# Feeding an attention stage up to eight units ahead, around the window in which expert weights arrive

## The chip, the cores and the metric

The kernel runs on one core of a Trainium2 chip. The metric is the device time of one execution in microseconds, the median over several executions of the same program.

## The reference

A linear attention with a decaying state (batch 4, 8 heads, 768 tokens, head size 48) is followed by a mixture of experts that sends every token to one of 8 experts (384 to 1024 to 384). Cut to what matters:

```python
for t in range(S):                                   # attention, state is (B, H, D, D)
    cur = einsum('bhd,bhe->bhde', u * k[t], v[t])
    y[t] = einsum('bhd,bhde->bhe', r[t], state + cur)
    state = w[:, :, None] * state + einsum('bhd,bhe->bhde', k[t], v[t])
x = y as (B*S, H*D)                                  # 3072 tokens of 384
e_idx = argmax(x @ w_gate + modality_bias[modality_id])
out[token] = gate[token] * (relu(x[token] @ w1[e]) @ w2[e])   # e = e_idx[token]
```

## The kernel before

**Units.** The attention works on 24 units of 128 tokens: unit i is batch `i % 4` of chunk `i // 4`. The main loop has one pass (step) for each unit, and several units are in flight in it. In step i TensorE forms the scores of unit i+1 (`scores`, `psc`, line 416), the outputs of unit i (`values`: `py` and the state's update `pst`, lines 446 to 464) and the bonus of unit i+1 (line 385). VectorE (DVE) prepares the keys of unit i+2 (`keys`, `kc`, line 376), masks the scores of unit i+1 (`causal`, line 422), and adds, scales and splits the output of unit i-1 (`token`, `low`, lines 472 and 521). ScalarE (ACT) and GpSimd (POOL) take other parts, and SyncE (SP) issues nearly all DMAs. All five engines run in program order, since the whole stage is written under a manual schedule.

**Feeds.** Each unit needs r and k with head dimensions on the partitions (`turned`, a DMA into one of four buffers `ud`, each with a half for r and a half for k, 192 KB a half) and k and v with tokens on the partitions (`lines`, a DMA of 384 KB into one of five buffers `kv`). For units in `TURNED`, 1 to 13, `turned` loads r alone; `keys_turned` gets the turned k by four TensorE transposes of the `kv` buffer into a PSUM tile `pkT` (line 339), which `keys` and nothing else then reads in the loop. In step i the kernel issues `turned(i + 5)` and `lines(i + 4)`, each behind a `pace`: SP reads a value that an engine has just made, so that the DMA is not issued before that time.

**Expert weights beside it.** From step 8 on the first expert's weights (3 MB) arrive in six pieces of 512 KB (`piece`, line 881, `raw`): three at the end of step 8, and one at the end of each of steps 9, 10 and 11. ACT sums their squares (`norm`), a small matmul adds these up (`scales`, `pww`, line 898; its result lies in the one-buffer PSUM pool that `pst` also uses), and the pieces are split into two half-precision parts, `whi` by ACT (line 914) and `wlo` by DVE (line 919): piece 0 at the end of step 11, pieces 1 and 2 at the end of step 12, pieces 3 to 5 at the end of step 13. From step 13 on every second step begins a tile of 128 tokens for that expert: `s_up` multiplies by `w1` (`phs`, line 973) in two halves, ACT and DVE turn each half into `hh` and `hl` (`s_high` line 977, `s_low` line 982), and in the next step `s_down` multiplies by `w2` (`pos`, lines 1047 and 1052), and ACT takes the result (line 933).

**PSUM.** The pool `ps_a` has four buffers of one bank. The transposed keys `pkT`, the two score tiles of a unit, both halves `phs` and `pos` all come from it in turn, each waiting until the tile that had its buffer four tiles ago has been read.

**After the loop** the remaining tiles go through the experts in a loop of jobs (from line 1397), which takes the span from about 200 us to its end.

In step i, the order of the calls that matter here is: feeds (step 0 only), `keys_turned(i+2)`, `scores(i+1)`, the first half of `s_up` or `s_high` and the first half of `s_down`, `token(i-1)`, `taken(i)`, `turned(i+5)`, state, `s_low` of the second half, `decay(i+3)`, `carry(i+2)`, `keys(i+2)`, `factor(i-1)`, `lines(i+4)`, `causal(i+1)`, `low(i-1)`, `values(i)`, the second half of `s_up` or `s_down`, logits and planned work (weight pieces, `norm`, splits).

Of the kernel before, what the change touches and what calls it, by code (L numbers as in the profile page):

```python
# [9 lines left out]
F32 = mybir.dt.float32  # L10
# [11 lines left out]
NPR = H // 2  # L22
NT = B * S
DM = H * D
# [6 lines left out]
WC = DC * F  # L31
# [11 lines left out]
DENSE = 6  # L43
FADED = range(4, 14)
SHARED = range(9, 14)
TURNED = range(1, 14)

NE = 9
EARLY = 3
# [8 lines left out]
LOW, TOP = 64 - D, 64 + D  # L58
# [3 lines left out]
class _Kernel:  # L62
# [251 lines left out]
    def turned(self, i):  # L314

        b, c = self.units[i]
        n = NPR * P
        ud = self.ud[i % len(self.ud)]
        m = n if i in TURNED else 2 * n
        self.nc.sync.dma_start(ud[LOW:TOP, :m], self.pd[b * NCH + c].rearrange("j d n -> (j d) n")[:, :m])  # L320
        self.ctx_.setdefault(i, {}).update( rT=ud[:, :n].rearrange("p (a t) -> p a t", a=NPR), kT=ud[:, n:].rearrange("p (a t) -> p a t", a=NPR))

    def lines(self, i, q=None):

        b, c = self.units[i]
        u = self.ctx_.setdefault(i, {})
        u["kz"] = self.kv[i % len(self.kv)]
        kv = u["kz"][:, LOW:]
        qs = slice(0, 2) if q is None else slice(q, q + 1)
        self.nc.sync.dma_start(kv.rearrange("p (q d) -> p q d", q=2)[:, qs], self.pt[b * NCH + c].rearrange("p (q d) -> p q d", q=3)[:, ::2][:, qs])  # L330
        u.update(k=kv[:, :DM], v=kv[:, DM:])

    def keys_turned(self, i):

        if i in TURNED:
            u = self.ctx_[i]
# [723 lines left out]
    def run(self):  # L1060
        nc, tc, m = self.nc, self.tc, self.m
        units = self.units = [(b, c) for c in range(NCH) for b in range(B)]
        NU = len(units)
# [14 lines left out]
        self.wf = m.tile([P, 1], F32, name="wf", bufs=1)  # L1078
        self.meta = m.tile([P, 2], F32, name="fac", bufs=1), m.tile([P, 2], I32, name="ids", bufs=1)
        self.mt, m2 = [m.tile([P, 2, 4], I16, name=f"mt{q}", bufs=1) for q in range(2)]  # L1080
        self.slot = {}
        junk = m.tile([P, WQ], F16, name="junk", bufs=1)
        groups = {}
# [15 lines left out]
        def chain(*gs):  # L1099
            for g in gs:  # L1100
                yield from g
# [37 lines left out]
        def route(i, d, f, *args):  # L1139
            for lo, hi in GROUPS:  # L1140
                if hi - 1 + d == i and lo in groups:
                    f(groups[lo], *args)

        def each(i, *fs):
            for f in fs:
                if live(i):
                    f(i)


        def fill(n=1):  # L1150
            while n and fills:
                g = fills.pop(0)
                if next(g, fills) is not fills:
                    fills.append(g)
                    n -= 1

        for i in range(NU - 1):
            if i == 0:
                each(i + 5, self.turned)
                each(i + 4, self.lines)  # L1160
            each(i + 2, self.keys_turned)
            each(i + 1, self.scores)
            if i + 1 > EARLY:
                each(i + 1, self.own_keys)
            route(i, 3, lambda u: fills.append(self.choose(u)))
            route(i, 5, lambda u: fills.append(chain(self.place(u), self.ahead(ahead[u["lo"]], u)) if u["lo"] in ahead else self.place(u)))
            up, down = ups.get(i), ups.get(i - 1)
            if up is not None:
                self.s_up(up, 0)
            if down is not None:  # L1170
                self.s_high(down, 1)
                self.s_down(down, 0)
            self.token(i - 1) if i else None
            if ups.get(i - 2) is not None:
                self.s_take(ups[i - 2])
            if i and i - 1 == self.grp["lo"]:
                groups[i - 1] = self.grp
            fill()
            each(i, self.taken) if i else None
            each(i - 1, self.settled_state)  # L1180
            if 0 < i < NU - 5:
                self.pace(self.ctx_[i]["d"])
                each(i + 5, self.turned)
            for j in range(2):
                each(i - 1, lambda i: self.state(i, j))
                fill()
            if down is not None:
                self.s_low(down, 1)
                self.s_due(down)
            begin.get(i, lambda: None)()  # L1190
            late = i >= NU - 3
            for k in range(1 if late else 2):
                for d in (6, 7):
                    route(i, d, self.send, 1)
                if k == 0:
                    each(i + 3, self.decay)
            if ups.get(i - 2) is not None:
                self.s_give(ups[i - 2])
            each(i + 2, self.carry)
            route(i, 4, self.sign)  # L1200
            each(i + 2, self.keys)
            if i + 2 <= EARLY:
                self.own_turned(i + 2)
            if i:
                fac = self.factor(i - 1)
                for _ in fac:
                    fill()
                if i < NU - 4:
                    self.pace(self.ctx_[i - 1]["g"]["sx"][:, self.ctx_[i - 1]["at_g"] :])
                    each(i + 4, self.lines)  # L1210
            self.own(i, 0)
            each(i - 1, self.high)
            mid.get(i, lambda: None)()
            for j in range(2):
                each(i + 1, lambda i: self.causal(i, j))
                fill()
            self.own(i, 1)
            if late:
                for d in (6, 7):
                    route(i, d, lambda u: (self.rest(self.ctx_[i]["dv"][:1, DM - 1 :]), self.send(u, 1)))  # L1220
            each(i - 1, self.low)
            if up is not None:
                self.s_high(up, 0)
                self.s_low(up, 0)
            fill()
            each(i - 1, self.flip)
            fill()
            self.values(i)
            if up is not None:
                self.s_up(up, 1)  # L1230
            if down is not None:
                self.s_down(down, 1)
            for p in range(2):
                for h in range(2):
                    c, r = divmod(i + 1 - 2 * p - h, B)
                    if r == 0 and 0 < c < NCH - 1:
                        self.fade(c, slice(2 * p, 2 * p + 2), range(2 * h, 2 * h + 2))
            if any(hi - 1 + d == i for lo, hi in GROUPS for d in (4, 5)):
                fill(99)
            route(i, 2, self.logits)  # L1240
            route(i, 4, self.count)
            for f in at.get(i, ()):
                f()
            for k in turns.get(i, ()):
                self.s_turn(k)
# [4 lines left out]
        i, j = NU - 2, NU - 1  # L1250
# [206 lines left out]
```

## Time and profile before

| | |
|---|---|
| median of 3 runs | 359.08 us (358.05 to 360.82) |
| the profiled execution | 358.22 us, its span 356.4 us |
| PE (matmul) busy | 337.7 us, 95% |
| PEld (weight load) busy | 273.0 us, 77% |
| DVE busy | 221.8 us, 62% |
| ACT busy | 173.4 us, 49% |
| POOL busy | 153.7 us, 43% |
| mean granted TensorE clock | 0.979 |

The span runs from the first to the last instruction. Rows of a timeline give the start in us from the span's start, the length in us, the engine, the line of the program, the operation, and what it writes and reads (buffer numbers left out); instructions of one kind that follow one another are merged, with their count behind an x. A bracket at the end gives the idle time ahead of it and what ended it. Rows of a list of waits give who waited, for whom, the total in us, how often, and the longest. Ends of matmuls are modelled. A share of busy time is a mean over stages with different limits.

### The profile page before, as it was taken

To read this page: it belongs to the slowest core of one execution; us is meant where nothing else is said; L and a number is where in the kernel's file an instruction comes from. 1 tells how busy PE (TensorE), PEld (TensorE's weight loads), DVE (VectorE), ACT (ScalarE), POOL (GpSimd) and SP (SyncE) were. 2 spreads that over 40 slices of the span, in tenths; PEclk is the share of its full clock that TensorE was granted. 3 is DMA by queue.
4 is the path that set the end of the run, shared out by engine and by line. 5 is a ranking of instruction groups with operands and counts; after the bars stand their busy time and mean duration, and the time that the engine had idled before them with its cause. 6 is when DMAs were issued, how large, how long until landed. Compare 5 with 4: busy or idle time off the path is not lost. (4 is left out here: it accounts for less than half of the span.)

```text
span 356.4 us, 15193 instructions
## 1 busy us (share of the span) xinstructions
PE 337.7 (95%) x5453; PEld 273.0 (77%) x5453; DVE 221.8 (62%) x745; ACT 173.4 (49%) x459; POOL 153.7 (43%) x231
## 2 busy tenths in 40 slices
PE   8999999799899999999998999998999999999893
PEld 3888998698769788887876777775788887777671
DVE  7978999489797978684658632258223232323850
ACT  8677675646847648465531122255222224552911
POOL 8986868646646765342267311112111210211121
PEclk9999999858999999999999999999999999999999
DMA  6875769999739998572335531126621121112110
GB/s 180 231 172 149 173 141 289 246 260 219 188 112 205 253 275 218 110 183 82 69 113 180 203 67 44 44 59 208 209 60 44 44 60 29 44 44 66 32 47 4
DMA packets 60796, 47.72 MB, mean 134 GB/s; under 512 B 46920, under 2 KB 54359, under 8 KB 60496
## 3 DMA queue, kind: packets, MB, share of 16 engines
q1 hardware_dynamic: 57552, 37.65, 45.0%
q0 software_dynamic: 3200, 9.47, 7.6%
q8 instruction: 30, 0.49, 0.6%
q14 instruction: 14, 0.11, 0.1%
HBM read 25.83 MB, written 11.83 MB: 106 GB/s over the span
## 5 line engine op out<-in xcount | busy, mean ns | idle before, releaser
L973 PEld LDWEIGHTS <-whi 128*128 128x128 f16 x1248 | 72.4, 98 | 4.0 <-issue 1.0
L1047 PEld LDWEIGHTS <-hh 128*128 128x128 f16 x416 | 37.4, 98 | 36.0 <-ACT hh L977 9.9
L973 PE MATMUL phb<-mxT,whi 128*128 128x128 f16 x768 | 50.8, 219 | 0.0
L402 ACT ACTIVATE dv<-kv,d 128x48 f32<-128x48 f32 x172 | 43.1, 325 | 3.9 <-issue 2.2
L977 ACT ACTIVATE hh<-phb 128x256 f16<-128x256 f32 (+1 forms) x48 | 21.5, 455 | 41.2 <-PE po L1047 19.4
L363 POOL TENSOR_TENSOR rk<-rc,kc 112x512 f32<-112x512 f32 x20 | 25.8, 1288 | 29.6 <-DVE ebx L301 13.3
L973 PEld LDWEIGHTS <-wlo 128*128 128x128 f16 x624 | 37.7, 98 | 0.0
L982 DVE SCALAR_TENSOR_TENSOR hl<-phb,hh 128x256 f16<-128x256 f32 (+1 forms) x48 | 24.1, 512 | 20.5 <-ACTq L1387 8.4
L1057 DVE TENSOR_SCALAR fac<-mt,wf 128x1 f32<-128x1 f32 x17 | 3.6, 213 | 50.9 <-DVEq L1387 30.7
L422 DVE TENSOR_TENSOR at<-psc,mask 128x512 f32<-128x512 f32 x48 | 31.7, 682 | 3.4 <-PE psc L416 3.2
L942 POOL TENSOR_TENSOR seenb<-otb,putb 128x1 int32<-128x1 int32 x16 | 3.0, 190 | 70.3 <-ACTq L1387 56.9
L351 POOL TENSOR_TENSOR rc<-ud,powr 128x512 f32<-128x512 f32 (+1 forms) x27 | 32.0, 1192 | 2.9 <-DMA ud<-in_pd 1.8
L1047 PE MATMUL po<-whi,hh 128*128 128x384 f16 x136 | 29.4, 328 | 3.2 <-ACT hh L977 2.3
L1052 PEld LDWEIGHTS <-hl 128*128 128x128 f16 x208 | 19.7, 98 | 13.8 <-issue 1.4
L641 POOL DMA_INDIRECT rows<-row,posi x24 | 25.0, 1042 | 11.0 <-DVE pr L718 3.8
L973 PE MATMUL phb<-mxT,wlo 128*128 128x128 f16 x384 | 29.3, 219 | 0.0
L1047 PE MATMUL po<-wlo,hh 128*128 128x384 f16 x136 | 28.0, 326 | 1.1 <-DVE wlo L919 1.1
L416 PE MATMUL psc<-rc,kc 48*64 48x128 f32 (+1 forms) x768 | 28.9, 288 | 0.1
L933 ACT ACTIVATE otb<-po,fac 128x384 f32<-128x384 f32 x16 | 9.3, 579 | 37.1 <-PE phb L973 35.0
L453 PE MATMUL py<-kv,at 128*64 128x48 f32 x768 | 27.3, 225 | 0.0
L973 PE MATMUL phs<-mxT,whi 128*128 128x128 f16 x432 | 27.2, 219 | 0.0
L416 PEld LDWEIGHTS psc<-rc,kc 64*64 64x64 f32 (+1 forms) x768 | 22.5, 140 | 5.5 <-issue 2.6
(265 smaller groups left out, 666.8 us busy)
## 6 DMA issues: line engine op xcount, KB each, us to landing
kv<-in_pt SPq DMA_DIRECT2D x21, 384.0 KB
raw<-in_w SPq DMA_DIRECT2D x12, 512.0 KB
ud<-in_pd SPq DMA_DIRECT2D x11, 384.0 KB
raw<-in_w SPq DMA_DIRECT2D x2, 1536.0 KB, 6.2
ud<-in_pd SPq DMA_DIRECT2D x13, 192.0 KB
rows<-pad SPq DMA_DIRECT2D x10, 193.0 KB
kv<-in_pt SPq DMA_DIRECT2D x6, 192.0 KB
rows<-row,posi POOLq DMA_INDIRECT x24
```

The lines of the kernel that those rows point to most:

```text
L351: nc.gpsimd.tensor_mul(u["rc"][:, s], u["rT"][:, s], self.powr[:, s])
L363: nc.gpsimd.tensor_mul(u["rk"][:TOP], u["rc"][:TOP], u["kc"][:TOP])
L402: nc.scalar.activation(u["dv"][:, sl], u["v"][:, sl], AF.Copy, scale=u["d"][:, h : h + 1])
L416: nc.tensor.matmul(u["ps"][j][s, pr * P : (pr + 1) * P], u["kc"][r, pr, s], u["rc"][r, pr, :], start=True, stop=True)
L422: nc.vector.tensor_mul(u["at"][:, j * NPR : (j + 1) * NPR, :], u["ps"][j].rearrange("p (q t) -> p q t", q=NPR), self.mask.unsqueeze(1).to_ ...
L453: nc.tensor.matmul(py[t, sl], u["at"][:, j * NPR + pr, t], u["v"][:, sl], start=c == h == 0, stop=h == H - 1, skip_group_check=True)
L641: i = nc.gpsimd.indirect_dma_start(out=self.rows, out_offset=bass.IndirectOffsetOnAxis(ap=u["posi"][:, b : b + 1], axis=0), in_=u["row"][: ...
L973: self.nc.tensor.matmul(ph[:, q * P : (q + 1) * P], w[:, c0 : c0 + P], self.xT[:, xq, t * P : (t + 1) * P], start=i == q == 0, stop=i == l ...
L977: self.nc.scalar.activation(self.hh[:, f0 : f0 + fb, t * P : (t + 1) * P], p3, AF.Relu)
L982: self.nc.vector.scalar_tensor_tensor(self.hl[:, f0 : f0 + fb, r], p3, 0.0, self.hh[:, f0 : f0 + fb, r], ALU.max, ALU.subtract)
L1047: self.nc.tensor.matmul(po[:, :DM], self.hh[:, f, t * P : (t + 1) * P], w[:, c0 : c0 + DM], start=n == q == f == 0, stop=False)
L1052: self.nc.tensor.matmul(po[:, :DM], self.hl[:, f, t * P : (t + 1) * P], self.whi[:, c0 : c0 + DM], start=False, stop=f == FB - 1)
```

## The change

Three tables say in which step which feed is issued, instead of `i + 5` and `i + 4`. The loads of r for units up to 17 go into eight half buffers: a unit's r takes the first or the second half of `ud[i % 4]` by turns, which the k of those units no longer needs, since `TURNED` now reaches to unit 17 and their k is turned by TensorE. k and v of units 9 to 12 go into four spare places: the memory of `hh` and `hl` and the second halves of `whi` and `wlo`, whose first 16 columns are zeroed by four small memsets after the setup; the units from 13 on go round the five `kv` buffers with a number lowered by four. In steps 9 to 12 no feed and no `pace` for one is issued.

```diff
-TURNED = range(1, 14)
+TURNED = range(1, 18)
+SPARE = range(9, 13)
+FEEDS = {0: (5,), 1: (6,), 2: (7, 8), 3: (9,), 4: (10, 11), 5: (12,), 6: (13, 14), 7: (15,), 8: (16, 17)}
+LINES = {0: (4,), 1: (5,), 2: (6, 9), 3: (7,), 4: (8, 10), 5: (11,), 6: (12, 13), 7: (14,), 8: (15, 16), 13: (17,)}
...
         ud = self.ud[i % len(self.ud)]
         m = n if i in TURNED else 2 * n
+        if i in TURNED:
+            ud = ud[:, i // 4 % 2 * n :]
...
-        u["kz"] = self.kv[i % len(self.kv)]
+        k = i if i < SPARE.start else i - len(SPARE)
+        u["kz"] = self.spare[SPARE.index(i)] if i in SPARE else self.kv[k % len(self.kv)]
...
+        self.spare = [t.bitcast(F32)[:, : LOW + 2 * DM] for t in (self.hh.rearrange("p f t -> p (f t)"), self.hl.rearrange("p f t -> p (f t)"), self.whi[:, WC:], self.wlo[:, WC:])]
+        for t in self.spare:
+            nc.vector.memset(t[:, :LOW], 0.0)
...
         for i in range(NU - 1):
+            feeds, lines = FEEDS.get(i, (i + 5,) if i > SPARE.stop - 1 else ()), LINES.get(i, (i + 4,) if i > SPARE.stop else ())
...
-            if 0 < i < NU - 5:
+            if 0 < i < NU - 5 and feeds:
                 self.pace(self.ctx_[i]["d"])
-                each(i + 5, self.turned)
+                for k in feeds:
+                    self.turned(k)
...
-                if i < NU - 4:
+                if i < NU - 4 and lines:
                     self.pace(self.ctx_[i - 1]["g"]["sx"][:, self.ctx_[i - 1]["at_g"] :])
-                    each(i + 4, self.lines)
+                    for k in lines:
+                        self.lines(k)
```

Step 0 issues its feeds ahead of everything else in the same way.

More of the change, by code (lines that the diff above doesn't have):

```diff
@@ L319, in turned @@
         m = n if i in TURNED else 2 * n
+        if i in TURNED:
+            ud = ud[:, i // 4 % 2 * n :]
         self.nc.sync.dma_start(ud[LOW:TOP, :m], self.pd[b * NCH + c].rearrange("j d n -> (j d) n")[:, :m])
-        self.ctx_.setdefault(i, {}).update( rT=ud[:, :n].rearrange("p (a t) -> p a t", a=NPR), kT=ud[:, n:].rearrange("p (a t) -> p a t", a=NPR))
+        self.ctx_.setdefault(i, {}).update(rT=ud[:, :n].rearrange("p (a t) -> p a t", a=NPR), kT=ud[:, n : 2 * n].rearrange("p (a t) -> p a t", a=NPR) if i not in TURNED else None)
     def lines(self, i, q=None):
@@ L1180, in run @@
             each(i - 1, self.settled_state)
-            if 0 < i < NU - 5:
+            if 0 < i < NU - 5 and feeds:
                 self.pace(self.ctx_[i]["d"])
-                each(i + 5, self.turned)
+                for k in feeds:
+                    self.turned(k)
             for j in range(2):
@@ L1207, in run @@
                     fill()
-                if i < NU - 4:
+                if i < NU - 4 and lines:
                     self.pace(self.ctx_[i - 1]["g"]["sx"][:, self.ctx_[i - 1]["at_g"] :])
-                    each(i + 4, self.lines)
+                    for k in lines:
+                        self.lines(k)
             self.own(i, 0)
```

## The prediction

> **What bounds the kernel now.** I read the stages first, as busy time of each engine in chosen stretches (start and end, length, then busy microseconds of PE, PEld, DVE, ACT and POOL with their counts, the granted clock, DMA share, GB/s). The steps named below are the passes of the main loop; step i is at unit i.
>
> ```profile
> span 356.4 us, 15193 instructions
> PE 337.7 (95%) x5453; PEld 273.0 (77%) x5453; DVE 221.8 (62%) x745; ACT 173.4 (49%) x459; POOL 153.7 (43%) x231
> 16.00:64.00 48.00, 47.77 (x1170) 42.47 (x1164) 42.27 (x128) 33.69 (x122) 37.79 (x38) 1.00 0.75 185
> 66.43:68.95 2.52, 0.01 (x2) 0.00 (x1) 0.46 (x3) 2.52 (x9) 1.27 (x1) 0.92 1.08 91
> 68.95:82.21 13.26, 13.26 (x184) 11.95 (x186) 9.27 (x29) 6.13 (x15) 6.87 (x8) 0.50 1.14 262
> 82.21:105.41 23.20, 21.18 (x432) 17.90 (x428) 21.07 (x52) 14.64 (x36) 13.75 (x12) 1.00 0.77 180
> 105.41:176.00 70.59, 70.18 (x1437) 60.18 (x1437) 52.99 (x187) 43.22 (x138) 34.21 (x43) 1.00 0.74 175
> 65.14:68.55 3.41, 1.29 (x35) 1.11 (x34) 1.71 (x9) 2.28 (x8) 1.61 (x2) 1.00 1.24 174
> 89.03:92.45 3.42, 1.87 (x50) 1.68 (x48) 2.11 (x12) 1.85 (x7) 0.51 (x2) 1.00 0.97 242
> ```
>
> PE is full from 16 to 64 us and again from 105 to 176. Between them lie the two losses that earlier feeds could remove: 2.52 us with no matmul, and then 13.26 us in which PE is full but at half clock, so that 6.6 us of its work is lost. The clock fell at 68.55 (0.92 over the second stretch) and rose at 82.2. The last two rows are windows of 3.41 us: PE was busy 1.29 us (38%) in the one before the clock fell and 1.87 us (55%) in one after which it held. So I take a 3.4 us window with 38% or less of matmul time as one that halves the clock here.
>
> The list of waits, the queue of SP and PE's order of time say what the 2.5 us were:
>
> ```profile
> PE pkT L339 <- DMA kv<-in_pt: 2.5, 1, 2.5
> 56.63 1.47 SPq L881 DMA_DIRECT2D raw<-in_w  x3
> 58.80 0.40 SPq L330 DMA_DIRECT2D kv<-in_pt  x1
> 60.90 0.63 PE L339 MATMUL pkT<-id,kv 128*112 128x128 f32 x4
> 61.46 1.10 PE L416 MATMUL psc<-rc,kc 64*64 64x128 f32 x32
> 65.81 0.62 PE L385 MATMUL pst<-uw,rk 112*64 112x2 f32 x15
> 68.95 1.10 PE L339 MATMUL pkT<-id,kv 128*112 128x128 f32 x4 [2.51 <-DMA kv<-in_pt]
> ```
>
> k and v of unit 13 were issued at 58.80, behind three weight pieces of 512 KB, and landed 10 us later. Under the change they are issued in step 6, so this wait goes. A full-speed step without expert work is 60.90 to 66.43: 5.5 us, of which the transposes take 0.56 and the rest 4.97.
>
> **What is late next: DVE.** From here on DVE has more than PE. Its order of time (a value in brackets is the idle time ahead and what ended it):
>
> ```profile
> 66.79 0.19 DVE L573 SCALAR_TENSOR_TENSOR er<-dl,idxf 128x32 f32<-128x32 f32 x1
> 71.90 0.18 PE L898 MATMUL pww<-wssq,onesb 128*128 128x3 bf16 x1
> 72.12 0.16 DVE L901 TENSOR_REDUCE wtotw<-pww 128x1 f32<-128x3 f32 x1 [5.14 <-PE pww L898]
> 78.05 0.55 DVE L472 TENSOR_TENSOR py<-py,dv 128x384 f32<-128x384 f32 x1
> 79.20 0.20 DVE L607 TENSOR_TENSOR pr<-pr,base 128x32 f32<-128x32 f32 x1 [0.60 <-PE pr L599]
> 85.13 3.99 DVE L919 SCALAR_TENSOR_TENSOR wlo<-raw,ws,whi 128x1024 f16<-128x1024 f32 x2
> L919 DVE SCALAR_TENSOR_TENSOR wlo<-raw,ws,whi x2: 1273/2035/2797, 85.1 to 87.8; 128x1024 f16<-128x1024 f32 x2
> 89.04 0.55 DVE L472 TENSOR_TENSOR py<-py,dv 128x384 f32<-128x384 f32 x1
> 90.63 0.17 PE L898 MATMUL pww<-wssq,onesb 128*128 128x3 bf16 x1 [1.55 <-ACT st L507]
> 95.45 4.97 DVE L919 SCALAR_TENSOR_TENSOR wlo<-raw,ws,whi 128x1024 f16<-128x1024 f32 x3 [0.60 <-ACT whi L914]
> 101.38 0.68 DVE L982 SCALAR_TENSOR_TENSOR hl<-phs,hh 128x512 f16<-128x512 f32 x1
> ```
>
> DVE, in program order, stands still for 5.14 us behind the late PE and then runs almost without a break to 102. With the wait gone, step 11's transposes start at 66.4, scores at 66.95, and `pww` 1.04 later (61.46 to 62.50 was the pitch of the same 32 matmuls), at 68.0; DVE resumes at 68.2, 3.9 us earlier. The 0.60 us before L607 and 0.1 to 0.2 more also go. So DVE's chain moves up by **4.7 us** and no more: the pair of splits starts at 80.4, L472 of step 13 at 84.3, the split of three ends at 95.7, and L982 ends at 102.06 - 4.7 = 97.3. What cannot move further stays: the splits, one of 1.27 and one of 2.80 us, the second stretched while POOL works.
>
> PE could move up 2.5 + 6.6 = 9.1 us, so it runs into DVE in step 13. Its own times: step 11 ends at 66.95 + 4.97 + 0.3 for the counting = 72.2; step 12, with the new transposes, at 77.8; transposes and scores of step 13 at 79.4.
>
> ```profile
> 86.90 1.51 PE L973 MATMUL phs<-mxT,whi 128*128 128x128 f16 x24
> 88.25 0.83 PE L973 MATMUL phs<-mxT,wlo 128*128 128x128 f16 x12
> 96.46 0.75 PE L544 MATMUL pr<-wghl,xT 128*128 128x16 f16 x24
> 97.14 1.10 PE L416 MATMUL psc<-rc,kc 64*64 64x128 f32 x32
> 98.17 1.15 PE L1047 MATMUL pos<-whi,hh 128*128 128x384 f16 x6
> 100.48 0.32 PE L1047 MATMUL pos<-wlo,hh 128*128 128x384 f16 x1 [0.34 <-DVE wlo L919]
> 101.38 0.88 PE L446 MATMUL py<-st,rc 112*64 112x96 f32 x16
> 105.41 1.10 PE L416 MATMUL psc<-rc,kc 64*64 64x128 f32 x32
> ```
>
> The `whi` half of the first expert matmuls then ends at 80.8; the `wlo` half needs the first split of the pair, done at 80.4 + 2.8 = 83.2 (a wait of 2.4 us), and ends 0.75 later at 83.95. Next in PE's queue is `pww`, which had waited 1.55 us already: its PSUM tile is free only after DVE's L472 and L390 and ACT's copy of the state, 1.59 us after L472 began (89.04 to 90.63). That is 85.9: a wait of 1.95 us. So PE has 0.75 us of matmul in 5.1 us, and nearly every position of a 3.41 us window on it has one window at 38% or less. **I expect the clock to be halved again, in step 13.** Behind the waiting PE stand everything of units 13 and 14; DVE does not wait for them until step 14.
>
> **The change part by part.**
> ```profile
> L98 DVE MEMSET kv<- x5: 72/72/72, 1.0 to 1.1; 128x16 f32 x5
> L376 DVE TENSOR_TENSOR kc<-pkT,powk x13: 669/680/692, 9.8 to 72.6; 112x512 f32<-112x512 f32 x13
> L376 DVE TENSOR_TENSOR kc<-ud,powk x12: 572/681/911, 6.1 to 154.8; 112x512 f32<-112x512 f32 x10, 112x256 f32<-112x256 f32 x2
> ```
>
> - *Earlier feeds.* Steps 2 to 8 issue eleven loads of r and eleven of k and v where seven of each stood: 905 KB in a step of some 5.5 us where it was 576. The DMA share of 0.75 in 16 to 64 leaves room; each load is asked for two steps or more ahead of its use. Cost 0, bounded by the 2.5 us that a late feed has cost. In steps 9 to 12 SP has two issues of about 0.4 us fewer and the weight pieces have the DMA to themselves; ACT waits less for them, which hides behind DVE.
> - *Other buffers.* The four small memsets (72 ns each by L98's row) lie on DVE before the first step while PE is full, 0.3 us if that cover were gone; `hh`, `hl`, `whi`, `wlo` are first written in step 13, after units 9 to 12 are done: no wait.
> - *Sixteen transposes.* 0.56 us a unit. In steps 12, 13 and 14 they lie in PE's waits for DVE or in the half-clock stretch that I count below; unit 17's 0.56 is on the path. `kc` is read from PSUM instead of SBUF: 680 against 681 ns, 0. Four loads of 192 instead of 384 KB: 0, no wait of before ends in them after step 11.
> - *A PSUM tile more.* `ps_a` has four buffers. In step 14 `pkT16`, two score tiles and `phs0_1` are alive when `pos0` wants one, so PE's L1047 must now wait for DVE's L982, which reads `phs0_1`. Before, L1047 began at 98.17 and L982 ended at 102.06, so 3.9 us of cover is gone: L1047 cannot begin before 97.3. Behind it wait L446 of unit 14 and all after it. Its 16 matmuls are 2.6 us without their wait of 0.34 (98.17 to 101.38 is 3.2), so L446 cannot come before 99.9, against 101.38: at most 1.5 us of gain passes this point, 0.9 with unit 17's transposes. In step 15 `phs1_0` waits likewise for ACT to take `pos0`; ACT is idle then, 0 to 1.8 us, taken as 0.
>
> *Sum.* From 85.9 to the scores of step 14 PE has 97.14 - 90.63 = 6.5 us of work. At half clock for 13.65 us (four windows, as now from 68.55 to 82.2), begun at about 84.5, it has done 6.1 of it by 98.1 and all of it by 98.5; with `pkT16` scores start at 99.05, L1047 at 100.1 (L982, free of PE but for the logits, is done by then), L446 at 102.7, which is 1.3 late; with unit 17's transposes 1.85. Begun at 86.4 it is 2.6. PE is full from there to 176, so nothing is made up: **+1.2 to +2.6, taken +1.9 us**. The execution profiled took 358.22 us (span 356.4 and 1.8 around it), the median of three is 359.08; on the median that is **361.0**.
>
> Of the clock the rows say that it stayed at 0.50 for 13.26 us with PE full throughout. The Trainium skill (TensorE: Matmul & The Clock Gate, Part 1, on the clock gate) has full speed return after one busy window of about 3.4 us. By that rule the second halving would cost a quarter, and the sum would be rival 1's; the trace speaks against it.
>
> **The rivals.** All on the median.
> 1. *The clock comes back sooner.* Half speed for one or two windows: PE is back before 97.3, and the PSUM wait decides: -0.9 to +0.5, 358.2 to 359.6. Against it: PE was full for 13.26 us at 0.50.
> 2. *No halving at all.* The gaps of 2.4 and 1.95 us are too short or fall well: the PSUM wait decides, from 94.0 (85.9 + 7.54 from `pww` to L1047, 90.63 to 98.17, + 0.56) to 97.3, and the clock survives it too: -0.9 to -2.0, 357.1 to 358.2. Against it: 2.5 us of gap sufficed at 66.4. The Trainium skill (TensorE: Matmul & The Clock Gate, "Why this matters for your kernels") warns of idle gaps over about 3 us, by which step 13 would keep its clock. The trace differs, with 2.52 us.
> 3. *Slower: the halving falls on the PSUM wait.* Step 13 keeps the clock, PE stands those 3.3 us before L1047, and the clock falls there for 13.65 us in which PE alone sets the pace: 6.8 - 0.9 = +4 to +5.9, 363.1 to 365.0. It decides if step 13 has no window at 38% or less, for instance when both its splits take 1.27.
> 4. *DVE is lighter than thought.* If all five splits took 1.27 us (9.0 us become 6.4), L982 ends 2.6 earlier and the gain is 3.6 to 5: 354 to 355.5. For it: POOL's timing decides the stretching; against: POOL follows DVE's `kc` as before.
> 5. *A feed comes late in steps 2 to 8*, or the wait for unit 13 stays: +2 to +8. Against: the share of 0.75.
>
> **How the numbers follow.** Forecast 0.45; rival 1 0.14; 2 0.11; 3 0.13; 4 0.12; 5 0.05. About 1% (3.6 us) is what a measurement here tells from no change. Faster by more: rival 4, 0.12. Slower by more: rival 3, most of 5 and the tail of the forecast, 0.13 + 0.04 + 0.03 = 0.20. Within: 0.68. Leaving out rivals 4 and 5 and the upper edge of 3, the range is 356.8 to 364.7.
>
> **What would show it.** No idle PE before `pkT13` and clock 1.00 at 69 us; L901 of step 11 at about 68.2; PE waiting on DVE's L919 and then on ACT's L507 in step 13; a clock of 0.50 starting between 84 and 87 (forecast) or near 97 to 99 (rival 3); L1047 of step 14 released by L982. I am wrong if DVE's splits in steps 12 and 13 begin much earlier than 80.4 and 90.7, if L1047 waits for nothing, or if a feed of units 6 to 12 ends a wait.

## The result, and the profile after

The changed kernel takes 361.06 us (median of 22 runs, 357.55 to 364.36), the kernel before 357.96 us (22 runs): a ratio of **1.0081, 95% interval 1.0053 to 1.0109**. The forecast was 361.0 us. (The ratios leave out executions over 1.5% above the fastest of the same kernel, so they differ a little from the quotients of the medians.) The profiled execution took 362.01 us, its span 360.2.

The page's head, then the same kind of stretches as before the change (start and end, length, busy microseconds of PE, PEld, DVE, ACT and POOL with counts, granted clock, DMA share, GB/s):

```profile
span 360.2 us, 15212 instructions
PE 338.2 (94%) x5469; PEld 273.3 (76%) x5469; DVE 220.5 (61%) x749; ACT 173.6 (48%) x459; POOL 153.3 (43%) x231
```

```profile
16.00:60.25 44.25, 44.23 (x1065) 39.01 (x1065) 39.15 (x113) 31.04 (x114) 34.39 (x34) 1.00 0.99 207
60.25:63.66 3.41, 2.03 (x57) 1.77 (x53) 2.46 (x11) 0.00 (x0) 3.06 (x4) 1.00 0.96 207
63.66:67.07 3.41, 3.41 (x53) 3.05 (x54) 1.53 (x6) 2.49 (x8) 2.94 (x4) 0.50 1.11 390
67.07:87.55 20.48, 18.19 (x406) 16.16 (x403) 18.12 (x59) 14.22 (x33) 12.75 (x13) 1.00 0.89 167
87.55:90.97 3.42, 1.65 (x47) 1.56 (x48) 2.14 (x10) 1.85 (x7) 0.51 (x1) 1.00 0.42 122
90.97:97.79 6.82, 6.82 (x79) 6.54 (x75) 6.19 (x9) 4.86 (x7) 6.27 (x5) 0.50 0.58 140
97.79:108.04 10.25, 9.86 (x179) 7.58 (x177) 7.98 (x28) 5.76 (x19) 2.94 (x4) 1.00 0.45 113
```

The long stretch at half clock from 68.55 to 82.2 is gone. In its place stand two shorter ones: one window at 63.66, and two from 90.97 to 97.79, which lie in step 13, where the forecast put them. The DMA share of the first stretch has risen to 0.99, from 0.75 between 16 and 64 us. The list of waits from 58 to 108 us, PE's rows (who waited for whom, total, times, longest):

```profile
PE pww L904 <- ACT st L513: 2.2, 2, 2.0
PE pr L550 <- DMA xT<-row: 1.4, 1, 1.4
PE phs L979 <- DMA mxT<-rows: 1.2, 1, 1.2
PE pos L1053 <- DVE hl L988: 0.4, 1, 0.4
```

The wait for `kv` of unit 13 is no longer in it. New are a wait of the logits for a transposing load, the forecast wait of `pww`, and the forecast wait of `pos0` for VectorE. (Lines moved by 3 to 6: L339 is now L345, L416 L422, L472 L478, L507 L513, L884 L890, L898 L904, L901 L907, L919 L925, L973 L979, L982 L988, L1047 L1053.) In order of time, picked rows:

```profile
51.74 0.97 SPq L325 DMA_DIRECT2D ud<-in_pd  x2
52.88 0.90 SPq L336 DMA_DIRECT2D kv<-in_pt  x2
53.91 1.22 SPq L532 DMA_TRANSPOSE xT<-row  x1
57.79 1.48 SPq L887 DMA_DIRECT2D raw<-in_w  x3
62.97 0.30 PE L550 MATMUL pr<-wghl,xT 128*128 128x16 f16 x6 [1.38 <-DMA xT<-row]
64.58 1.06 ACT L890 ACTIVATE junk<-raw 128x1024 f16<-128x1024 f32 x1 [4.50 <-DMA raw<-in_w]
72.06 0.16 DVE L907 TENSOR_REDUCE wtotw<-pww 128x1 f32<-128x3 f32 x1 [1.45 <-PE pww L904]
89.32 0.17 PE L904 MATMUL pww<-wssq,onesb 128*128 128x3 bf16 x1 [2.00 <-ACT st L513]
94.79 2.74 PE L979 MATMUL phs<-mxT,whi 128*128 128x128 f16 x24
99.39 1.10 PE L422 MATMUL psc<-rc,kc 64*64 64x128 f32 x32
100.88 1.14 PE L1053 MATMUL pos<-whi,hh 128*128 128x384 f16 x6 [0.39 <-DVE hl L988]
108.04 1.10 PE L422 MATMUL psc<-rc,kc 64*64 64x128 f32 x32
```

Step 8 now issues 1152 KB of feeds (51.74 and 52.88) where it issued 576, and the transposing load of unit 7's rows (53.91) and the first weight pieces (57.79) stand behind them in the queue. The logits that need that load start their last six matmuls at 62.97, 9 us after it was issued. From there PE works without a wait of more than 0.2 us up to `pww` of step 11, but 3.41 us of that time at half clock, which is 1.7 us of work lost. ACT, which sums the squares of the first piece, meanwhile stands 4.50 us until 64.58 (1.29 before the change), and its part of step 10 is late too. So L907 of step 11 comes at 72.06, where it stood before (72.12): VectorE gained nothing. From there to the scores of unit 16 it goes

| | before | after |
|---|---|---|
| L907 of step 11 (L901 before) | 72.12 | 72.06 |
| from it to `pww` of step 13 | 18.51 | 17.26 |
| from `pww` to the scores of unit 15 | 6.51 | 10.07 |
| from these to the scores of unit 16 | 8.27 | 8.65 |
| scores of unit 16 | 105.41 | 108.04 |

The loss is in the third row: 3.56 us, of which the transposes of unit 16 are 0.56; the other 3.0 go with the two windows at half clock (in e9 below, with the clock kept, the same stretch takes 7.00). Of the 3.8 us between the two spans 2.6 are thus placed. The other 1.2 arise behind the scores of unit 16, in one wait: at 211.45 the first matmuls of the loop of jobs (`pha`, L979) wait 1.41 us for a transposing load. They do not wait in the profiles of before, e2 and e12, and in e9, e10 and e11 0.8 to 1.3 us; what makes that load late was not traced.

### The profile page after: what moved, and what is told of

Read it like the earlier page. It is cut to its first block, busy times and chain, and to the rows that moved or that the text cites. A ratio compares the mean times of both kernels' runs of the same rounds, so it can differ in the third digit from the quotient of the medians.

```text
span 360.2 us, 15212 instructions
## 1 busy us (share of the span) xinstructions
PE 338.2 (94%) x5469; PEld 273.3 (76%) x5469; DVE 220.5 (61%) x749; ACT 173.6 (48%) x459; POOL 153.3 (43%) x231
## 5 line engine op out<-in xcount | busy, mean ns | idle before, releaser
L979 PEld LDWEIGHTS <-whi 128*128 128x128 f16 x1248 | 73.5, 99 | 6.6 <-issue 2.2
L1053 PEld LDWEIGHTS <-hh 128*128 128x128 f16 x416 | 37.5, 98 | 36.1 <-ACT hh L983 10.4
L979 PE MATMUL phb<-mxT,whi 128*128 128x128 f16 x768 | 50.8, 219 | 0.0
L408 ACT ACTIVATE dv<-kv,d 128x48 f32<-128x48 f32 x156 | 39.0, 325 | 3.9 <-issue 2.2
L979 PEld LDWEIGHTS <-wlo 128*128 128x128 f16 x624 | 38.0, 98 | 0.0
L988 DVE SCALAR_TENSOR_TENSOR hl<-phb,hh 128x256 f16<-128x256 f32 (+1 forms) x48 | 24.1, 511 | 20.5 <-issue 7.3
L1053 PE MATMUL po<-whi,hh 128*128 128x384 f16 x136 | 29.6, 327 | 3.2 <-ACT hh L983 2.3
L979 PE MATMUL phs<-mxT,whi 128*128 128x128 f16 x432 | 28.4, 224 | 1.2 <-DMA mxT<-rows 1.2
L979 PE MATMUL phb<-mxT,wlo 128*128 128x128 f16 x384 | 29.3, 219 | 0.0
L422 PE MATMUL psc<-rc,kc 64*64 64x128 f32 (+1 forms) x768 | 28.2, 283 | 1.1 <-POOL rc L357 0.9
L1053 PE MATMUL po<-wlo,hh 128*128 128x384 f16 x136 | 28.0, 326 | 1.1 <-DVE wlo L925 1.1
L422 PEld LDWEIGHTS psc<-rc,kc 48*64 48x64 f32 (+1 forms) x768 | 21.6, 136 | 6.9 <-issue 2.3
L1058 PE MATMUL po<-whi,hl 128*128 128x384 f16 x136 | 24.9, 326 | 0.8 <-PEq L1467 0.8
```

The costliest lines, as they stand in the source:

```text
L408: nc.scalar.activation(u["dv"][:, sl], u["v"][:, sl], AF.Copy, scale=u["d"][:, h : h + 1])
L422: nc.tensor.matmul(u["ps"][j][s, pr * P : (pr + 1) * P], u["kc"][r, pr, s], u["rc"][r, pr, :], start=True, stop=True)
L979: self.nc.tensor.matmul(ph[:, q * P : (q + 1) * P], w[:, c0 : c0 + P], self.xT[:, xq, t * P : (t + 1) * P], start=i == q == 0, stop=i == l ...
L988: self.nc.vector.scalar_tensor_tensor(self.hl[:, f0 : f0 + fb, r], p3, 0.0, self.hh[:, f0 : f0 + fb, r], ALU.max, ALU.subtract)
L1053: self.nc.tensor.matmul(po[:, :DM], self.hh[:, f, t * P : (t + 1) * P], w[:, c0 : c0 + DM], start=n == q == f == 0, stop=False)
L1058: self.nc.tensor.matmul(po[:, :DM], self.hl[:, f, t * P : (t + 1) * P], self.whi[:, c0 : c0 + DM], start=False, stop=f == FB - 1)
```

## The experiments

Four kernels shared a chip each time. The second chip, that of e5 to e8, runs the kernel before in 351.8 us and not in 358, so ratios are compared and not microseconds. In the traces that difference arises behind the steps looked at here: e2 on the first chip and e6 on the second reach the scores of unit 16 at 106.27 and 105.98, and take 250.1 and 246.7 us from there. The table has what each run's trace shows of the same four steps; the sections below take them in turn.

| kernel | ratio to before | 95% | L907, step 11 | to `pww` | to scores 15 | to scores 16 |
|---|---|---|---|---|---|---|
| after | 1.0081 | 1.0053-1.0109 | 72.06 | 17.26 | 10.07 | 8.65 |
| e1 feeds behind the transpose | 1.0105 | 1.0053-1.0156 | 74.15 | 17.65 | 8.53 | 11.60 |
| e2 pww in `pst`'s tile | 1.0059 | 1.0020-1.0097 | 69.29 | 17.27 | 11.50 | 8.21 |
| e3 e1 and e2 | 1.0104 | 1.0055-1.0154 | 75.15 | 17.27 | 8.54 | 10.19 |
| e4 before, weights later | 1.0060 | 1.0026-1.0095 | 74.28 | 17.89 | 6.50 | 8.27 |
| e5 16 not transposed | 1.0027 | 0.9987-1.0067 | 68.22 | 17.28 | 8.04 | 8.21 |
| e6 light step 8 | 1.0080 | 1.0040-1.0121 | 69.09 | 17.27 | 11.42 | 8.20 |
| e7 e5 and e6 | 1.0013 | 0.9966-1.0060 | 70.77 | 17.26 | 6.50 | 8.70 |
| e8 e7, L907 later | 0.9997 | 0.9955-1.0039 | 67.76 | 17.26 | 9.57 | 8.21 |
| e9 after, PE kept at work | 1.0099 | 1.0065-1.0132 | 69.36 | 17.28 | 7.00 | 14.25 |
| e10 e7, pww in `py`'s tile | **0.9936** | 0.9897-0.9974 | 68.99 | 16.41* | 6.41 | 8.39 |
| e11 e10 and e9 | 0.9968 | 0.9933-1.0002 | 68.97 | 16.43* | 6.41 | 8.39 |
| e12 before, PE kept at work | 0.9975 | 0.9938-1.0012 | 71.12 | 17.35 | 6.51 | 8.26 |

(* to L452 of unit 13, which stands behind `pww` and there waits for L907.)

**e1.** Theory: the feeds of step 8 push the transposing load back. The order of the two is turned round.

```diff
-            if 0 < i < NU - 5 and feeds:
+            if 0 < i < NU - 5 and feeds and i != 8:
...
-                if i < NU - 4 and lines:
+                if i < NU - 4 and lines and i != 8:
...
             each(i - 1, self.flip)
+            if i == 8:
+                for k in feeds:
+                    self.turned(k)
+                for k in lines:
+                    self.lines(k)
```

> The changed kernel with one order turned round: in step 8 the four feeds (r of units 16, 17; k v of 15, 16; 1152 KB) are issued behind the transposing load of unit 7's rows (L532) and not ahead of it. Theory (the feeds push that load back): it lands by about 58 us instead of 62.9, the logits of step 9 (L550) wait for nothing where they waited 1.4 us, the clock is not halved near 64, and L907 of step 11 comes at about 69 instead of 72.1. What follows is the meeting with VectorE in step 13, so of the 3.1 us (1.4 of wait, 1.7 lost in one window at half clock) most is given back there: 358.5 to 361 us against 361.06. Rival (the stall of step 9 has another cause, for instance the weight pieces behind it): L550 waits 1 us or more as before, 360.5 to 361.5.

The logits no longer wait for the load (0.19 us, put down to issue). But the same bytes now stand nearer to the weight pieces, and ACT's wait for the first piece grew from 4.50 to 6.44 us, in the order of time:

```profile
65.99 1.06 ACT L890 ACTIVATE junk<-raw 128x1024 f16<-128x1024 f32 x1 [6.44 <-DMA raw<-in_w]
68.03 1.22 PE L465 MATMUL pst<-st,wd 112*112 112x96 f32 x8 [3.19 <-ACT st L513]
```

PE then waits 3.19 us for the state that ACT copies behind that sum, two windows at half clock follow, and L907 is two microseconds later than in the changed kernel. The theory's first half fits (the delay went with the order from the load to the piece), though in e2 and e9, with the order not turned, the logits did not wait for the load either. The expectation of 358.5 to 361 does not hold: 361.85.

**e2.** Theory one: VectorE sets the end of step 14. Theory two: the clock does.

```diff
-        pt = (pool or self.ps_s).tile([P, 512], F32, tag=tag, name="pw" + key)
+        pt = (pool or self.ps_s).tile([P, 512], F32, tag=tag, name="pw" + key) if key != "w2" else self.ctx_[12]["pst"][:, 448:]
```

> The changed kernel with the sum for the second weight scale (pww of step 13, L904) written into free columns of the PSUM tile of unit 12's state and not into a tile of its own, so that it need not wait for that tile's readers. Theory one (VectorE sets the end of step 14): the 2.0 us wait at L904 goes, and PE waits the longer for VectorE before L1053 of step 14, whose L988 comes at the same time: 360.0 to 361.0 us. Theory two (the clock is what costs): with that wait gone no window of step 13 is thin enough, the half clock of 91 to 97.8 (3.4 us of PE work lost) does not come, and the time is 357.0 to 358.5.

The edit took nothing away. The write into free columns waited for the tile's readers all the same, as PE's order of time has it:

```profile
86.56 0.17 PE L904 MATMUL pst<-wssq,onesb 128*128 128x3 bf16 x1 [2.71 <-ACT st L513]
```

The window in which that wait lies, and the stretch behind it:

```profile
82.94:86.36 3.42, 0.90 (x14) 0.64 (x12) 2.65 (x4) 0.82 (x4) 1.53 (x2) 1.00 0.49 116
86.36:96.60 10.24, 10.04 (x120) 9.67 (x120) 9.10 (x16) 5.91 (x12) 6.52 (x5) 0.50 0.47 136
```

So e2 serves as a second look at the changed kernel (1.0059, its interval and that of the changed kernel overlap). Here no load came late in step 9, L907 stood at 69.29, and `pww` at 86.56, 2.8 us earlier than in the other profile and 4.1 earlier than before the change. Three windows at half clock, 86.36 to 96.60, took the 4.1 us and more: from `pww` to the scores of unit 15 PE took 11.50 us, and these came at 98.06, 0.9 us later than before the change. So with no late load the advance was lost in step 13 all the same; whether the load matters to the time, e6 tests.

**e3.** Both edits.

> Both edits of the two kernels before this one together. If the two waits are the cause of all that the changed kernel loses (1.4 and 2.0 us, and three windows at half clock, 5.1 us of PE work), scores of unit 16 come near 103 us where they came at 108.0, and the time is 355 to 357 us. If VectorE sets the pace from step 12 on, L988 of step 14 ends at 97 to 98 instead of 100.7 and the time is 357.5 to 359. If the clock falls in step 13 all the same (the waits for the splits alone do it), 359.5 to 361.

1.0104, as e1, since the second edit changed nothing: 361.93 us, above all three ranges of the expectation, which had counted on it.

**e4.** The kernel before, with weight pieces 1 to 3 a step later (piece 4 kept its place in step 10, so three pieces are moved and not the four of the expectation): the wait for unit 13 is to go without one earlier feed.

```diff
-            plan(O + max(q - 2, 0), first(q))
+            plan(O + (1, 1, 2, 2, 3)[q - 1], first(q))
```

> The kernel before the change, with four of the first expert's six 512 KB weight pieces issued later: pieces 1 and 2 at the end of step 9 and not of step 8, pieces 3 and 4 at the end of step 10 (3 was at the end of step 9), the last one where it was. Nothing else is changed: no earlier feeds, no added transposes, no other buffers. Theory (that wait of 2.5 us and the half clock after it were the loss of step 11, and the meeting with VectorE in step 13 gives most of it back): k and v of unit 13 land before step 11, L339 of step 11 waits for nothing, and the time stays within 356.5 to 359.5 (before: 358). Rival one (what PE gains there is kept): 350 to 354. Rival two (later pieces make the norms and so VectorE's scale late by the time that they are delayed): over 359.5.

The wait for `kv` went, and its place was taken at once by the norms of the later pieces, as in the second rival, though the time is below the figure given for that (358.7 us, where the median of before is 358.33 on this chip; the ratio is 1.0060). In the order of time:

```profile
70.39 1.06 ACT L884 ACTIVATE junk<-raw 128x1024 f16<-128x1024 f32 x1 [4.16 <-DMA raw<-in_w]
74.07 0.16 PE L898 MATMUL pww<-wssq,onesb 128*128 128x3 bf16 x1 [4.41 <-ACT st L507]
```

**e5 to e7.** Unit 16 is left as before the change (no fifth tile in step 14), step 8 is made light, and both.

```diff
-TURNED = range(1, 18)
+TURNED = [i for i in range(1, 18) if i != 16]     # e5, e7
-FEEDS = {..., 8: (16, 17)}
+FEEDS = {..., 8: (17,), 11: (16,)}                # e5, e7;  e6: 8: (16,), 11: (17,)
-LINES = {..., 8: (15, 16), 13: (17,)}
+LINES = {..., 8: (15,), 12: (16,), 13: (17,)}     # e6, e7
```

> The changed kernel with unit 16 alone as it was before the change: its k is not transposed on TensorE but loaded turned beside r (384 KB, issued in step 11; step 8 issues 192 KB less). So step 14 has four tiles alive in the PSUM pool ps_a and not five. In all six traces so far VectorE takes 28.0 to 29.3 us from L907 of step 11 to L988 of step 14 (L901, L982 before), and the scores of unit 16 start 4.0 us after L988 without the added transposes and 8.0 to 9.4 us after it with them. Theory one (the wait of pos0 for VectorE's L988 orders PE's step 14 behind VectorE): 4.0 us again, and the time falls from 361.1 to 356.5 to 358. Theory two (those 4 us are half clock, not the tile): 8 us as in the changed kernel, 360 to 361.5.

> The changed kernel with a lighter step 8: k and v of unit 16 are issued in step 12 and r of unit 17 in step 11, so that step 8 issues 576 KB as before the change and not 1152. Theory (step 8's feeds hold back the three weight pieces and the transposing load behind them; ScalarE waits 3 to 5 us for the first piece in step 10, and all of step 10 and pww of step 11 behind it): ScalarE's wait for raw at L890 is under 1 us, L907 of step 11 comes at 68 to 69.5 instead of 72.1 to 74, L988 of step 14 at 96.5 to 98, and with the wait for the PSUM tile left as it is the time is 357.5 to 359. Rival (VectorE's 28 to 29 us do not hang on L907, or another wait takes over): 360 to 361.5.

> The two edits before this one together: unit 16 not transposed (r and k of it issued in step 11), k and v of unit 16 issued in step 12, so step 8 issues 192 KB of r and 384 KB of k and v. If pww of step 11 and the tile of step 14 are the two places, their gains add: L907 at 68 to 69.5, L988 at 96.5 to 98, scores of unit 16 at 100.5 to 102 and the time 353 to 355. If half clock in step 13 eats the gain as the prediction had it: 357 to 359.

e6 did what was expected of its loads (ACT's wait for the first piece 1.61 us, L907 at 69.09) and gained nothing: 1.0080. Like e2 it lost the advance in three windows at half clock (11.42 us from `pww` to scores 15). e5 and e7 gained, to 1.0027 and 1.0013, less than expected; their intervals still touch that of the changed kernel. From e6 to e7 unit 16 goes back to its turned load, and the order of two small loads changes with it: 0.67% or 2.4 us, of which the transposes on PE are 0.56. In e5 one window was halved, in e7 none, though both waited at `pww`. PE's order of time in e5, and then in e7:

```profile
85.50 0.17 PE L904 MATMUL pww<-wssq,onesb 128*128 128x3 bf16 x1 [2.72 <-ACT st L513]
93.54 1.10 PE L422 MATMUL psc<-rc,kc 64*64 64x128 f32 x32
```

```profile
88.03 0.17 PE L904 MATMUL pww<-wssq,onesb 128*128 128x3 bf16 x1 [2.71 <-ACT st L513]
94.53 1.10 PE L422 MATMUL psc<-rc,kc 64*64 64x128 f32 x32
```

The two waits are of one length, but the windows lie otherwise. In e5 nearly the whole wait fell into the window from 82.82 to 86.23, which kept 0.73 us of matmuls (22%), and the clock fell behind it. In e7 the clock changed only at 349.30. Counted back from there in steps of 3.413 us (67.07 and 90.97, two changes of clock in the changed kernel's profile, are seven of them apart), the edge of a window at 86.48 cuts the wait in two, and neither part made a window thin enough:

```profile
83.06:86.48 3.42, 2.07 (x34) 1.78 (x32) 3.39 (x5) 1.37 (x3) 2.25 (x2) 1.00 1.09 275
86.48:89.89 3.41, 1.86 (x50) 1.72 (x49) 2.10 (x12) 1.85 (x7) 0.56 (x2) 1.00 0.57 155
```

The 4 and 8 us from L988 to the scores of unit 16, by which e5's expectation set its theories apart, turned out to be no sign of the tile: they are 5.5 in e5, 4.5 in e7 and 7.6 in e8, which has no fifth tile in step 14 either but two windows at half clock. So theory two, as far as that number goes. That the tile is an obstacle too is shown by e9, and by e1 and e3, where PE stood 1.94 and 1.93 us before `pos0` for L988.

**e8.** In step 13 VectorE's part of the second weight scale stands behind `keys`.

```diff
-            begin.get(i, lambda: None)()
+            begin.get(i, lambda: None)() if i != 13 else None
...
             each(i + 2, self.keys)
+            begin.get(i, lambda: None)() if i == 13 else None
```

> As the kernel before this one, and in step 13 VectorE's part of the second weight scale (L907 and what follows it) stands behind the multiplication for kc of unit 15 (L382), not ahead of it, so that VectorE does not stand the 1.17 us there that it stood in every trace while the tile went from L478 by ScalarE and TensorE back to it. If VectorE sets the pace of steps 11 to 14, its chain from L907 of step 11 to L988 is 1.0 to 1.2 us shorter (27 to 28 us) and the time 0.8 to 1.2 below that of the kernel before this one (352 to 354). If TensorE or its clock sets it, no change from that kernel.

0.9997 against e7's 1.0013: the intervals do not tell them apart, but e8's lies below that of the changed kernel. In this trace L907 to L988 of step 14 took 27.4 us (28.0 in e7), and two windows were halved.

**e9.** The direct test of the clock: eight matmuls that nobody reads fill PE's wait in step 13 of the changed kernel.

```diff
         s[g] = self.ps_a.tile([P, 512], F32, tag="big", name=f"phs{k}_{g}")
+        for _ in range(8 if (k, g) == (0, 0) else 0):
+            self.nc.tensor.matmul(s[g], self.ones16, self.warm, start=True, stop=True)
```

> The changed kernel with eight matmuls of 128x512 f16 more (0.27 us each, 2.2 in all), whose result is thrown away: they write the tile phs0_0 ahead of its real matmuls in step 13 and so fill PE's wait for pww with work. In seven traces VectorE takes 17.3 us (18.5 before the change) from L907 of step 11 to pww of step 13, and from pww to the scores of unit 15 PE takes 6.5 us at full clock (7.1 with unit 16's transposes) and 8.0 to 11.5 us where one to three windows at half clock fall there. Theory (that half clock is what the changed kernel loses): with the fillers no window there is halved, scores of unit 15 come 24.4 us after L907 of step 11 where they came 27.3 after it, and the time is 0.6 to 1.2% below the changed kernel's: a ratio to before of 0.996 to 1.002 where it was 1.008. Rival one (VectorE or the fifth PSUM tile holds step 14 all the same): 1.005 to 1.010. Rival two (the fillers only move the wait): 1.008 and over.

PE's order of time, picked rows:

```profile
81.16 1.90 PE L1020 MATMUL phs<-warm 128*128 128x512 f16 x8
86.64 0.17 PE L904 MATMUL pww<-wssq,onesb 128*128 128x3 bf16 x1 [1.58 <-ACT st L513]
93.64 1.10 PE L422 MATMUL psc<-rc,kc 64*64 64x128 f32 x32
98.21 2.08 PE L1055 MATMUL pos<-whi,hh 128*128 128x384 f16 x6 [3.47 <-DVE hl L988]
```

The window of that last wait and the one behind it (columns as above):

```profile
93.23:96.65 3.42, 1.51 (x36) 1.09 (x35) 3.42 (x4) 0.75 (x2) 2.10 (x2) 1.00 0.16 58
96.65:100.06 3.41, 1.85 (x6) 0.87 (x7) 3.38 (x16) 2.52 (x9) 1.06 (x1) 0.50 0.36 115
```

The clock of step 13 was kept and the scores of unit 15 came at 93.64, 5.75 us earlier than in the profile of the changed kernel (2.7 of them because L907 came earlier, 3.1 with the clock). Then PE stood 3.47 us before `pos0` for VectorE's L988, with the fifth tile, and the clock fell there, for two windows (96.65 to 103.47). Scores of unit 16: 107.89. This is rival 3 of the prediction in its order of events, with two windows where it had four, and it cost as much as the halving that it replaced: 1.0099. The two obstacles stand one behind the other, and whoever removes the first meets the second.

**e10 and e11.** On top of e7, `pww` of step 13 goes into free columns of unit 13's `py`, whose buffer has been free for long; e11 adds e9's matmuls.

```diff
+            if half:
+                self.py13 = self.ps_y.tile([P, 512], F32, tag="y", name="py13")
-            for _ in self.scales_(key, slice(half, half + 1)):
+            for _ in self.scales_(key, slice(half, half + 1), pt=self.py13[:, 448:] if half else None):
...
-        py = u["py"] = self.ps_y.tile([P, 512], F32, tag="y", name=f"py{i}")
+        py = u["py"] = self.py13 if i == 13 else self.ps_y.tile([P, 512], F32, tag="y", name=f"py{i}")
```

> The kernel of e7 (unit 16 not transposed, step 8 light), and pww of step 13 is written into free columns of the tile py of unit 13, whose former reader is done long before, and not into a tile that ScalarE's copy of the state must leave first. So pww waits for nothing, VectorE goes from L478 to L907 without its 1.17 us, and the matmuls L452 of unit 13 wait only for L907. If VectorE and this loop set the pace, L907 of step 11 to L452 of step 13 falls from 17.4 to some 16.4 us and the time is 0.3% below e7's (ratio to before 0.997 to 0.999), more if the shorter wait keeps the clock. If the wait is only renamed, as in e2: 1.001.

> The kernel before this one with the eight fillers as well: light step 8, unit 16 not transposed, pww in py's tile, PE kept at work in step 13. If the three losses of step 13 and 14 are what is left (wait, half clock, tile), scores of unit 15 come 23 us after L907 of step 11 in every run, and the ratio to before is 0.988 to 0.994. If the clock was already kept by the shorter wait: the same as the kernel before this one.

PE's order of time in e10:

```profile
83.48 0.17 PE L904 MATMUL py<-wssq,onesb 128*128 128x3 bf16 x1
85.40 0.88 PE L452 MATMUL py<-st,rc 112*64 112x96 f32 x16 [1.75 <-DVE wtotw L907]
91.81 1.10 PE L422 MATMUL psc<-rc,kc 64*64 64x128 f32 x32
```

Its thinnest window of step 13:

```profile
82.03:85.45 3.42, 1.67 (x32) 1.54 (x29) 3.39 (x6) 0.82 (x3) 1.60 (x2) 1.00 1.15 258
```

In e10 `pww` waits for nothing, the wait behind it has shrunk to 1.75 us, the clock stayed, and the scores of unit 16 start at 100.20. **355.43 us, 0.9936 of before**: the version that beats both kernels (its interval ends at 0.9974, that of the changed kernel begins at 1.0053). It is more than the 0.3% under e7 that the wait alone was expected to give, but the two ran on different chips and their intervals overlap.

Not all of the lead reaches the end. Against e12, nearly the kernel before on the same chip, the scores of unit 16 come 3.0 us earlier (100.20 and 103.24), but the span ends only 0.5 us earlier (353.5 and 354.0). Of the difference 1.28 us are the wait of `pha` told above, and 1.09 a wait in step 15:

```profile
102.40 1.50 PE L979 MATMUL phs<-mxT,whi 128*128 128x128 f16 x24 [1.09 <-ACT ots L939]
```

e11 has the same times at the same places (91.81 and 100.20), so with the clock kept the extra matmuls add nothing; its ratio is within e10's interval and above the expected 0.994.

**e12.** The kernel before, with nine such matmuls in the 2.5 us of the wait in step 11.

```diff
             pt = self.ps_a.tile([P, 512], F32, tag="big", name=f"pkT{i}")
+            for _ in range(9 if i == 13 else 0):
+                self.nc.tensor.matmul(pt, self.ones16, self.warm, start=True, stop=True)
```

> The kernel before the change with nine fillers of 128x512 f16 (2.4 us) ahead of the transposes of unit 13 in step 11, in the 2.5 us in which PE waits for k and v. The wait itself stays, but no window is empty and the clock should stay at 1.00 from 66 to 82 us, where 6.6 us of PE's work were lost at half clock. If PE sets the pace there, the time is 1.5 to 2% below before (ratio 0.980 to 0.985). If VectorE does, as the prediction has it, PE only waits longer in step 13: pww comes 17.3 to 18.5 us after L901 of step 11 as ever, and the ratio is 0.997 to 1.000, or 1.002 to 1.010 if the clock is then halved in step 13 instead.

The stretch that was at half clock before, and then a row of PE's order of time:

```profile
68.55:82.21 13.66, 10.68 (x229) 9.22 (x227) 10.95 (x35) 7.38 (x18) 7.96 (x10) 1.00 1.08 267
```

```profile
88.47 0.17 PE L900 MATMUL pww<-wssq,onesb 128*128 128x3 bf16 x1 [1.75 <-ACT st L509]
```

The stretch that ran at half clock before the change ran at 1.00, PE had 3 us to spare in it, and the time fell by 0.25%, with an interval that contains no change. Between the profiles of before and of e12 (two chips) `pww` of step 13 moved 2.16 us up and the span's end 2.4, so about a third of the 6.6 us of PE work lost there in the kernel before reached the end, and the rest was hidden behind VectorE. The median says less than it seems to: the mean granted clock was 0.999 in this profile, but its median over the 12 executions was 0.990, against 0.986 in the kernel before on this chip, so most of them had windows at half clock all the same (one of 3.41 us in 355 lowers the mean by 0.005), and where is not on record. In the kernel before on this chip, the 12 executions that the ratio counts with a mean clock of 0.990 or more took 356.8 us on average, the 9 with 0.982 or less 359.1.

## Why the prediction was right, and where it was not

- **What is late next: right, and the firmest result.** From L907 of step 11 to `pww` of step 13 the prediction has 17.7 us (68.2 to 85.9); eight of the eleven rows of the table that end at `pww` have 17.26 to 17.28 and the other three up to 17.9, with the clock halved in between or not. e12 shows it from the other side: with the clock kept in step 11 the same way took 17.35.
- **`pww`'s wait: right.** Forecast 1.95 us for ACT's copy of the state, measured 2.00, and 2.7 in seven variants (e1 to e3, e5 to e8). The wait of 2.4 us for the first split of the pair did not come (0.26 at most, in e1); in its place `phs0_0` waited 1.23 us in the profile of after for a transposing load that the prediction did not consider.
- **The halving in step 13: right in place, wrong in size.** It came at 86 to 91 us in the changed kernel's profile and in e2, e5, e6 and e8 (forecast 84 to 87), and at 92.6 in e1 and e3, whose L907 was late. The term for its length, four windows, was too long: one to three, 1.5 to 4.4 us of PE work instead of 6.8. The sign taken for a halving, a window with 38% or less of matmul time, was too narrow: windows with 44% (e9 from 93.23), 48% and 60% (after, from 87.55 and 60.25) were followed by half clock too.
- **Earlier feeds at cost 0: the step that failed.** In the profiled run a transposing load and a weight piece came late behind them, and L907 stood at 72.06 where 68.2 was forecast. The prediction looked for late feeds and not for what stands behind the feeds in the queue. Of these 3.9 us 1.05 were there after the very first loads (scores of unit 1 at 12.22, 11.17 before the change), ahead of anything that the change moves. In e2 and e9, which have the same feeds, L907 stood at 69.3, so most of this cost comes and goes; in all three profiles ACT waited longer for the first piece, 2.73 to 4.50 us against 1.61 and 1.94 with the light step 8 of e6 and e10. It is not what makes the changed kernel slower: e6, without it, is at 1.0080.
- **The PSUM tile more: right in kind.** It waited 0.39 us in the profile of after, 1.94 and 1.93 in e1 and e3, and 3.47 in e9, where PE came early; rival 3 had reckoned 3.3 us. The wait of `phs1_0` for ACT in step 15, taken as 0, did not come in the profile of after, and was 1.1 us in e7, e10 and e11.
- **The sum** was +1.9 us and +2.9 was measured (0.81% of 357.96). In the profile the late L907 (+3.9) made up for the two missing windows (-3.4) and for the tile that hardly waited. That 361.0 met 361.06 is in part luck: these errors cancel, and the base of 359.08 was 1.1 us above the later median. Of the other rivals, 2 and 4 are excluded for the changed kernel by its traces (the clock fell, and the five splits took 8.2 us, 3.22 and 4.98, not 6.4); 1, a short halving, happened, without its gain.

The Trainium skill (TensorE: Matmul & The Clock Gate, Part 1) has full speed return after one busy window of about 3.4 us; the prediction held against it that the trace spoke of four. The runs have both and what lies between, with PE 97% busy or more: one window in e5, two in after, three in e2, four before.

What stays open is how often step 13 keeps its clock with the wait in place. Of the profiles with a wait of 2.0 to 2.7 us at `pww` only e7 kept it; the kernel before, e9, e10 and e12, with waits of 1.55 to 1.75 us at `pww` or right behind it, kept it too. Where the windows lie differs from execution to execution, and a profile shows one of many: over all 12 executions the median of the mean granted clock is 0.991 in e7, whose profile has 0.998, and 0.997 in e10. So e7's profile is one of its better executions, and e10 loses less to half clock in most of them.

## What to carry to other kernels

Before a wait is taken away, follow the engine that will be late next to the next place where the two meet, and price the wait there: here two more obstacles, a one-buffer PSUM tile and a fifth claim on four buffers, stood behind the first and had to go together. A load issued earlier is not free because its own consumer is far: what stands behind it in the queue, transposing loads and weights above all, can land later. Work lost at half clock is paid for only in part while another engine is late as well (about a third of 6.6 us between the profiles of before and e12), and filling a wait with idle matmuls bought nothing that could be told from no change (e12), nothing where the clock was kept anyway (e11), and nothing where a second obstacle stood behind the first (e9).

## Of the hardware, not expected

The share of matmul time in a 3.41 us window does not by itself say whether the clock is halved. Windows with 49% (e10 from 82.03) and 55% (before from 89.03, e7 from 86.48) kept it, but ones with 59% (e1, 99.44 to 102.85: 2.00 us) and 60% (after, 60.25 to 63.66: 2.03 us) were followed by half clock. In the window of after 40 of 57 matmuls have 2 to 16 columns, but in that of e1 only 19 of 55, and the others have 128; so short matmuls alone do not explain it, and what is counted stays open. A transposing load of 768 packets of 256 bytes released its reader 9 us after its issue behind 1152 KB of feeds (in e2 and e9, behind the same feeds, its reader did not wait); the Trainium skill (DMA: Bandwidth & Descriptors, "Queues, rings and completion order") says that descriptors are consumed in ring order on each DMA engine, and the wait in this trace fits that.
